# A quarter of the Q projection: plain matmuls in place of seven half-size products

## The chip, the cores and the metric

One core of one Trainium2 chip runs the whole program in a single launch. The metric is the device time in microseconds (us), given as the median of several executions. The engines are TensorE (PE in the profile, with its weight loads as PEld), VectorE (DVE), ScalarE (ACT), GpSimd (POOL), and SyncE (SP), whose queue issues most of the DMAs.

## The reference, cut to what matters

```python
x = A_x                                             # 1 x 2048 x 1024, bf16
# A: linear attention on layernorm(x), 32 heads of 32
q, k, v = split(layernorm(x) @ wqkv)                # wqkv 1024 x 3072
pq, pk = phi(q), phi(k)                             # phi(t) = (t + 1 if t > 0 else exp(t)) + 1e-6
kv = sum over tokens of pk * v ; z = sum over tokens of pk
o = (pq @ kv) / (pq . z + 1e-6)
h = x + o @ wo
# B: a two-layer MLP over the tokens of layernorm(h), with w1 (2048 x 3584), GELU, w2 (3584 x 2048)
out = h + B(layernorm(h))
```

The change lies in `q = layernorm(x) @ wq` and `pq = phi(q)` for 512 of the 2048 tokens, and in where intermediate sums are kept.

## The kernel before, in words

Tokens are handled in 16 tiles of 128; two tiles make a pair q = 0 to 7; four tiles make a block u = 0 to 3 of 512 tokens. The normalised tokens lie transposed in `xnT`.

**Seven products instead of eight.** For K of the pairs 2 to 7 and V of the pairs 1 to 7 (the rest of K and V is plain), a 256 x 1024 x 1024 product is done as a 2 x 2 block product with seven block multiplications (Strassen's scheme in Winograd's form). `Run` holds the seven, `p1` to `p7`; each is four matmuls of 128 x 512 into one PSUM bank. They need four sums of blocks of the weights (`w_sums`, t1 to t4, made once for each of K, V and Q) and four sums of blocks of the tokens (`x_sums`, s1 to s4, made for every pair); VectorE makes all of them. Product `p6` needs s2 and t2. ScalarE copies PSUM banks from one product to the next, and VectorE adds E, the bank of `p5`, to the banks after `p7` and `p3`.

**The rounds.** One round handles one pair: a K run, then a V run. `run_step` weaves the end of the run before (`p3`, `p4`) into the start of the next (`p1`, `p6`, `p2`, `p5`, `p7`). The same function fixes the order on VectorE and ScalarE: phi of a K result is two ScalarE instructions (`exp`, `relu`) and two on VectorE (`min` and `add`, then a sum). `late12` is the ScalarE pair and `dve12` the VectorE pair of the K result of `p3`. `after6` takes the layernorm statistics of a later token tile (`ln_stats`), `after5` finishes it (`ln_finish`: ScalarE `Ln` and `Exp`, VectorE `norm`, a transposing DMA), and `after7` makes the token sums of the next pair. An instruction given to `pin` stays behind the instruction traced before it on its engine; instructions without `pin` (the matmuls of `q_unit`, the memsets of `kv_ps`) are placed by the framework.

**Q.** For tokens 0 to 1023 and 1536 to 2047 the projection is plain: `q_unit` (in the rounds' gaps) and `q_held` (after the rounds) do one 128 x 512 block of Q with eight matmuls of 128 x 512, followed by the four instructions of phi. For tokens 1024 to 1535 (u = 2) two runs `QRun`, one for each half of the output columns, stand in round q = 5, each behind a K or V run. A `QRun` does seven products of eight matmuls of 128 x 256. Its four weight sums are made one by one on VectorE, behind the K runs of rounds 2 to 5 (`q_sums`). Its tokens come out in another order (`place`), and its phi of two of four results takes the relu on VectorE (`lean`).

**After the rounds.** The loop over `q_units[8:]` does the remaining plain Q blocks (16 here), and between them the denominators (`den`), their spreading over partitions through DRAM (`den_spread`), the folding of kv into wo (`fold`), the first weight loads and sums of B. Then the loop over the 16 token tiles seeds two PSUM banks with x (`seed`), adds the output matmuls (`out_mm`, 16 matmuls), copies and takes statistics (`out_evac`), and normalises (`normalize_h`). PSUM banks of these loops come in turn from a ring of five (`acc_tile`). The first banks of B (`psA`, `psB`) reuse the same memory.

Before, the sums of K lie in `shared_sb` (t2 to t4) and in place of one weight block (t1), those of V in `wo_sb` and likewise in place.

Of the kernel before, what the change touches and what calls it, by code (L numbers as in the profile page):

```python
# [10 lines left out]
P = 128  # L11
F32 = mybir.dt.float32
BF16 = mybir.dt.bfloat16
# [17 lines left out]
def kernel(  # L31
# [152 lines left out]
    def phi_parts(dst, src, n, pool, view=lambda t: t, lean=False):  # L184
        e_sb = pool.tile([P, n], BF16, tag="phi_e", name="e_sb")
        r_sb = None if lean else pool.tile([P, n], BF16, tag="phi_r", name="r_sb")

        def act():
            pin(nc.scalar.activation(e_sb[:], src, ACT.Exp))  # L189
            if not lean:  # L190
                pin(nc.scalar.activation(r_sb[:], src, ACT.Relu))

        def dve():
            pin(nc.vector.tensor_scalar(e_sb[:], e_sb[:], 1.0, PHI_EPS, ALU.min, ALU.add))  # L194
            if lean:
                pin(nc.vector.scalar_tensor_tensor(dst, view(src), 0.0, view(e_sb[:]), ALU.max, ALU.add))
            else:
                pin(nc.vector.tensor_tensor(dst, view(e_sb[:]), view(r_sb[:]), ALU.add))

        return act, dve  # L200
# [583 lines left out]
    with ExitStack() as actx:  # L784
        a3s = actx.enter_context(tc.tile_pool(name="a3s", bufs=4))
        hstat = actx.enter_context(tc.tile_pool(name="hstat", bufs=1))
        QT = ND // 2 * CW
        shared_sb = hstat.tile([P, 3 * QT + SW + (XRL + 1) * D], BF16, name="shared_sb")
        thirds = [shared_sb[:, i * QT:(i + 1) * QT] for i in range(3)]
        rd_sb = shared_sb[:, 3 * QT:3 * QT + SW].bitcast(FP16)  # L790
        xr_at = 3 * QT + SW
        xr_first = [shared_sb[:, xr_at + i * D:xr_at + (i + 1) * D] for i in range(XRL + 1)]
        assert (XRL + 1) * D >= 2 * QT
# [17 lines left out]
        with ExitStack() as a1:  # L811
# [7 lines left out]
            wo_parts = [wo_sb[:, 2 * t:2 * t + 2, :].rearrange("p a b -> p (a b)") for t in range(4)]  # L819

            def as_sums(flat):
                return [t.bitcast(FP16).rearrange("p (k c) -> p k c", c=CW) for t in flat]

            tv, tk = as_sums(wo_parts[0:3]), as_sums(thirds)
            tq = [
                t.bitcast(FP16).rearrange("p (k j f) -> p k j f", k=ND // 2, f=P)
                for t in (shared_sb[:, xr_at:xr_at + QT], shared_sb[:, xr_at + QT:xr_at + 2 * QT], wo_parts[3])
            ]
            spool = a1.enter_context(tc.tile_pool(name="spool", bufs=1))
# [101 lines left out]
            def with_sums(blocks, ts):  # L931
                return blocks, (blocks[1].bitcast(FP16), *ts)

            wq_b = wq_sb[:].rearrange("p (k two) (j par f) -> p k two j par f", two=2, par=2, f=P)
            kmov = with_sums(w_blocks(0), tk)
            vmov = with_sums(w_blocks(D), tv)
            qmov = with_sums([wq_b[:, :, k, :, c, :] for k in range(2) for c in range(2)], tq)

            def w_sums(mov, part):
                (b11, b12, b21, b22), (t1, t2, t3, t4) = mov  # L940
                for out, a, b in ((t3, b22, b12), (t1, b12, b11), (t2, b22, t1), (t4, b21, t2))[part]:
                    pin(nc.vector.tensor_tensor(out, a, b, ALU.subtract))

            xs_sb = spool.tile([P, 2, 4, hk2, P], FP16, name="xs")
# [5 lines left out]
            def x_sums(q, part=slice(0, 4)):  # L950
                a11, a12, a21, a22 = x_blocks(q)
                sm = xs_sb[:, q % 2]
                for out, a, b, op in (
                    (sm[:, 0], a21, a22, ALU.add), (sm[:, 1], sm[:, 0], a11, ALU.subtract),
                    (sm[:, 2], a11, a21, ALU.subtract), (sm[:, 3], a12, sm[:, 1], ALU.subtract),
                )[part]:
                    pin(nc.vector.tensor_tensor(out, a, b, op))  # L957

            class Run:
                def __init__(self, q, mov):  # L960
                    self.q = q
                    self.a11, self.a12, self.a21, self.a22 = x_blocks(q)
                    self.s1, self.s2, self.s3, self.s4 = (xs_sb[:, q % 2, t] for t in range(4))
# [82 lines left out]
            class KRun(Run):  # L1046
# [4 lines left out]
                lean = False  # L1051

                def view(self, t):
                    return t

# [3 lines left out]
                def evac(self, h, ps):  # L1059
                    self.phi[h, 0] = phi_parts(self.dst(h, 0), ps[:], CW, a2k, self.view)  # L1060
                    self.phi[h, 0][0]()

                def add(self, h, ps):
                    t = epool.tile([P, BANK], F32, tag="kt", name="kt")
                    pin(nc.vector.tensor_tensor(t[:], ps[:], self.E[:], ALU.add))
                    self.phi[h, 1] = phi_parts(self.dst(h, 1), t[:], CW, a2k, self.view, self.lean)
# [19 lines left out]
            class QRun(KRun):  # L1086
                lean = True

                def __init__(self, u, half):
                    self.u, self.half, self.phi = u, half, {}  # L1090
                    xv = xnT[:, :, u * SW:(u + 1) * SW].rearrange("p (k two) (r t f) -> p k two r t f", two=2, t=2, f=P)
                    self.a11, self.a12, self.a21, self.a22 = (xv[:, :, k, :, t, :] for t in range(2) for k in range(2))
                    self.s1, self.s2, self.s3, self.s4 = (
                        xs_sb[:, :, t].rearrange("p r k f -> p k r f") for t in range(4)
                    )
                    (self.b11, _, self.b21, self.b22), (self.t1, self.t2, self.t3, self.t4) = qmov

                def view(self, t):
                    return t.rearrange("p (j n) -> p j n", j=2)

                def mm(self, ps, lhs, rhs, start):
                    out = ps[:].rearrange("p (j r f) -> p j r f", j=2, f=P)
                    for j in range(2):
                        for k in range(hk2):
                            pin(nc.tensor.matmul(
                                out[:, j],
                                lhsT=rhs[:, k, 2 * self.half + j, :],
                                rhs=lhs[:, k],
                                start=(start and j == 0 and k == 0),
                                stop=(k == hk2 - 1),  # L1110
                                skip_group_check=True,
                            ))

                def dst(self, h, c):
                    n0 = self.u * SW + h * SW // 2
                    v = pqT[:, 4 * self.half:4 * self.half + 4, n0:n0 + SW // 2]
                    return v.rearrange("p (j two) n -> p j two n", two=2)[:, :, c, :]

            def run_step(n, prev, after6=None, after5=None, after7=None, fill=None, after3=None):
# [6 lines left out]
                if after3 is not None:  # L1126
                    after3()
# [11 lines left out]
                if n is not None:  # L1139
                    n.dve11()  # L1140
                if after5 is not None:
                    after5()
                if n is not None:
                    n.p7()
                prev.dve12()
# [115 lines left out]
            phi_dve((2, 0))  # L1261
            k_unit(2, 1)
# [16 lines left out]
            w_sums(kmov, slice(1, 3))  # L1279
# [3 lines left out]
            w_sums(vmov, slice(0, 1))  # L1283
# [5 lines left out]
            w_sums(vmov, slice(1, 3))  # L1289
# [13 lines left out]
            assert NSC == 4  # L1303
            q_units = [(u, j) for u in (0, 1, NSC - 1) for j in range(ND)]
# [17 lines left out]
            w_sums(kmov, slice(3, 4))  # L1322
            w_sums(vmov, slice(3, 4))
# [9 lines left out]
            q_sums = {2: slice(0, 1), 3: slice(1, 2), 4: slice(2, 3), 5: slice(3, 4)}  # L1333
            for q in range(2, NVP):
                runs = [KRun(q), VRun(q)]
                if q == 5:
                    runs = [runs[0], QRun(q // 2, 0), runs[1], QRun(q // 2, 1)]
                for n in runs:
                    kind = type(n).__name__[0]
                    i = {"K": 2 * q + 3, "V": 2 * q + 4}.get(kind, NS)  # L1340
# [5 lines left out]
                    def after5():  # L1346
                        if kind == "V":
# [6 lines left out]
                    def after7():  # L1354
                        if kind == "V" and q != 5 and q + 1 < NVP:
                            x_sums(q + 1)
                        if kind == "Q" and n.half == 1:
                            x_sums(q + 1, slice(0, 3))
                        if kind == "K" and q in q_sums:
                            w_sums(qmov, q_sums[q])  # L1360

                    def after3():
                        if type(prev) is QRun and prev.half == 1:
                            x_sums(q, slice(3, 4))

                    run_step(n, prev, after6, after5, after7, after3=after3)
                    prev = n
                if q == 6:
                    q_rows = wqkv_v.rearrange("p (k two) c -> p k two c", two=2)[:, :, 0, 0:D]
# [461 lines left out]
```

## Time and profile before

| what | value |
|---|---|
| median of 7 executions | 562.9 us (562.54 to 563.9) |
| the profiled execution: its own time, its span | 562.54 us, 560.8 us |
| TensorE busy | 552.4 us, 99% of the span, 3387 matmuls |
| TensorE weight loads busy | 320.2 us, 57% |
| VectorE busy | 441.9 us, 79% |
| ScalarE busy | 291.7 us, 52% |
| granted TensorE clock | 1.0 of full speed |
| chain that ended last | 85% TensorE, 5% VectorE, 2% ScalarE, 2% DMA |

The span runs from the first to the last instruction that the profile records; 1.7 us of the execution lie outside it. The end of a matmul is modelled: a line of four matmuls of 128 x 512 shows about 1.03 us although the next one can start 0.86 us after it. So the distance between two starts is what to read, and a waiting time that the profile shows on TensorE is shorter than the time lost.

The first 30 us load the first tokens and do the plain K and V, the rounds run from 41.5 to 138 us, the plain Q blocks from there to 179 us, the output projection to 235 us, and B from there to the end.

### The profile page before, as it was taken

How to read it: one execution, taken by the hardware profiler on the slowest of the kernel's cores; microseconds unless marked ns; L12 is line 12 of the kernel's file. 1: busy time of each engine (PE TensorE's matmuls, PEld its weight loads, DVE VectorE, ACT ScalarE, POOL GpSimd, SP SyncE). 2: the span in 40 equal slices, each digit the busy share in tenths (PEclk: the TensorE clock that was granted, in tenths of full speed). 3: DMA queues.
4: the chain of work that ended last, by engine and by line, in shares of the span. 5: the costliest groups of instructions: out<-in, count | busy, mean ns of one | idle time of the engine just before them, and what ended most of it. 6: DMA issues, size and time to landing. Idle time of an engine off the chain costs nothing.

```text
span 560.8 us, 8942 instructions
## 1 busy us (share of the span) xinstructions
PE 552.4 (99%) x3387; PEld 320.2 (57%) x3387; DVE 441.9 (79%) x858; ACT 291.7 (52%) x619; POOL 26.2 (5%) x36
## 2 busy tenths in 40 slices
PE   8999999999999999999999999999999999999997
PEld 3444446645444444456666666666444667667665
DVE  7798888664469689879989889897996879749746
ACT  5747767676677867645455565464310412413313
POOL 1000000000000000000000000000003103103111
PEclk9999999999999999999999999999999999999999
DMA  9933332310576992202240430413769659849434
GB/s 304 298 75 76 76 76 38 94 20 28 209 234 187 287 284 85 79 1 72 81 151 0 151 124 29 150 38 96 201 203 237 198 137 242 207 131 223 93 106 73
DMA packets 84443, 75.56 MB, mean 135 GB/s; under 512 B 15650, under 2 KB 76336, under 8 KB 84400
## 3 DMA queue, kind: packets, MB, share of 16 engines
q1 hardware_dynamic: 79632, 70.66, 42.2%
q0 software_dynamic: 4096, 3.68, 4.8%
q10 hardware_dynamic: 672, 0.66, 0.3%
q8 instruction: 26, 0.43, 0.3%
q14 instruction: 17, 0.14, 0.1%
HBM read 60.17 MB, written 11.67 MB: 128 GB/s over the span
## 4 chain that ended last, share of the span: by engine, by line
PE 85%; DVE 5%; ACT 2%; DMA 2%; issue 1%; DVEq 0%; ACTq 0%
PE psI L234 23%; PE psC L234 14%; PE acc_t L234 14%; PE psB L234 8%; PE psB L968 4%; PE psA L968 3%; PE psC L968 3%; PE psA L346 2%; PE psB L346 2%; PE acc_t L1294 2%; PE psE L968 2%; DMA wq<-in_B_w_dram 2%; PE psC L346 2%; PE psA L234 1%; PE psE L346 1%; DVE is L234 1%
## 5 line engine op out<-in xcount | busy, mean ns | idle before, releaser
L234 PEld LDWEIGHTS <-is 128*128 128x128 f16 x736 | 71.9, 98 | 31.6 <-DVE is L234 0.9
L234 PEld LDWEIGHTS <-sa 128*128 128x128 f16 x606 | 59.2, 98 | 27.5 <-issue 0.3
L234 PEld LDWEIGHTS <-wq 128*128 128x128 bf16 (+1 forms) x496 | 48.4, 98 | 28.9 <-issue 2.1
L234 PE MATMUL acc_t<-wo_sb,pqT 128*128 128x512 f16 x256 | 55.6, 379 | 0.0
L492 POOL DMA_DIRECT2D out_dram<-wq x28 | 24.4, 928 | 522.4 <-ACT wq L495 488.2
L234 PEld LDWEIGHTS <-pqT 128*128 128x128 bf16 x256 | 25.0, 98 | 30.5 <-issue 0.6
L234 DVE TENSOR_TENSOR t<-psI,t 128x256 f32<-128x256 f32 (+1 forms) x45 | 20.8, 475 | 22.2 <-PE psI L234 21.0
L234 PE MATMUL psC<-gs,wq 128*128 128x512 f16 x140 | 34.1, 379 | 0.0
L968 PEld LDWEIGHTS <-xs 128*128 128x128 f16 x208 | 19.7, 98 | 24.9 <-DVE xs L957 3.8
L194 DVE TENSOR_SCALAR e_sb<-e_sb 128x512 bf16<-128x512 bf16 x64 | 18.3, 286 | 19.1 <-ACT e_sb L189 19.0
L234 PE MATMUL psC<-hT,sa 128*128 128x512 f16 x112 | 31.2, 379 | 0.0
L234 PE MATMUL psI<-hi,is 128*128 128x256 f16 x200 | 30.0, 273 | 0.0
L234 PE MATMUL psB<-hT,sa 128*128 128x512 f16 x112 | 29.7, 379 | 0.0
L234 PE MATMUL acc_t<-xnT,wq_sb 128*128 128x512 bf16 x128 | 29.6, 379 | 0.0
L189 ACT ACTIVATE e_sb<-acc_t 128x512 bf16<-128x512 f32 x32 | 19.1, 597 | 18.7 <-PE acc_t L1294 9.4
L968 PE MATMUL psA<-wkv,xnT 128*128 128x512 bf16 x104 | 26.7, 379 | 0.0
L234 DVE BATCH_NORM_STATS2 hst<-acc_t 128x6 f32<-128x512 f32 x32 | 21.1, 689 | 6.4 <-ACT h_bf L234 6.4
L968 PEld LDWEIGHTS <-xnT 128*128 128x128 bf16 x156 | 15.3, 98 | 18.5 <-issue 0.8
L234 PE MATMUL psC<-hT,wq 128*128 128x512 f16 x96 | 24.6, 379 | 0.0
L234 DVE TENSOR_TENSOR e<-psI,es 128x256 f32<-128x256 f32 x20 | 8.5, 424 | 20.4 <-PE psI L234 20.4
L234 ACT COPY psI<-psI 128x256 f32<-128x256 f32 x50 | 18.0, 360 | 11.3 <-PE psI L234 9.4
L234 PE MATMUL psI<-gi,is 128*128 128x256 f16 x168 | 22.3, 273 | 0.4 <-DVE is L234 0.4
(242 smaller groups left out, 1129.8 us busy)
## 6 DMA issues: line engine op xcount, KB each, us to landing
wq<-in_B_w_dram SPq DMA_DIRECT2D x14, 1024.0 KB, 7.8
wq<-in_B_w_dram SPq DMA_DIRECT2D x12, 896.0 KB, 7.5
gs<-parked SPq DMA_DIRECT2D x9, 896.0 KB, 4.7
shared_sb<-rd_dram SPq DMA_DIRECT2D x32, 128.0 KB, 4.7
out_dram<-h_bf SPq DMA_DIRECT2D x16, 256.0 KB, 2.9
x_sb<-in_A_x_dram SPq DMA_DIRECT2D x15, 256.0 KB, 3.0
w2o<-in_B_w_dram SPq DMA_DIRECT2D x4, 896.0 KB, 10.7
out_dram<-wq POOLq DMA_DIRECT2D x28, 128.0 KB, 5.0
```

Of the source, the lines that this page charges most:

```text
L189: pin(nc.scalar.activation(e_sb[:], src, ACT.Exp))
L194: pin(nc.vector.tensor_scalar(e_sb[:], e_sb[:], 1.0, PHI_EPS, ALU.min, ALU.add))
L234: return (lambda *a, **kw: pin(op(*a, **kw))) if self.always or getattr(Held, self.key) else op
L346: pe.matmul(ps[:, cols], lhsT=lhs[:, k, :], rhs=mv(k)[:, cols], start=(start and k == 0), stop=(k == self.nk - 1), skip_group_check=True,)
L492: nc.gpsimd.dma_start(to, ot[:, a:b], accum_op=ALU.add)
L968: pin(nc.tensor.matmul(ps[:], lhsT=lhs[:, k, :], rhs=rhs[:, k, :], start=(start and k == 0), stop=(k == hk2 - 1), skip_group_check=True,))
L1294: nc.tensor.matmul(qp[:, 0:SW], lhsT=wq_sb[:, kt, j * P:(j + 1) * P], rhs=xnT[:, kt, u * SW:(u + 1) * SW], start=(kt == 0), stop=(kt == ND ...
```

## The change

The two `QRun` of round 5 go, with their four weight sums, the lean form of phi, the reordering of tokens and the DMA that reloads half of wq. The 512 tokens become eight more plain Q blocks in the loop after the rounds (24 in place of 16). The sums of K move to `pqT`, all four of V to `wo_sb`, so that no weight block is overwritten, and they are made in another order and at other places. In `run_step`, `dve12` moves from behind `p7` to a place ahead of `after5`. The buffers of reciprocals and of x get pools of their own. Denominators, spreads, scalings and the first loads of w1 get other places in the two loops after the rounds.

```diff
-            tv, tk = as_sums(wo_parts[0:3]), as_sums(thirds)
...
+            tv = wo_sb[:].rearrange("p (t a) (b c) -> p t (a b) c", t=4, c=CW).bitcast(FP16)
+            tk = pqT[:, ND - 4:ND, :].rearrange("p t (b c) -> p t b c", c=CW).bitcast(FP16)
...
-                for out, a, b in ((t3, b22, b12), (t1, b12, b11), (t2, b22, t1), (t4, b21, t2))[part]:
+                for out, a, b in ((t1, b12, b11), (t2, b22, t1), (t3, b22, b12), (t4, b21, t2))[part]:
                     pin(nc.vector.tensor_tensor(out, a, b, ALU.subtract))
...
-            class QRun(KRun):
...
                 prev.late12()
                 if n is not None:
                     n.dve11()
+                prev.dve12()
                 if after5 is not None:
                     after5()
                 if n is not None:
                     n.p7()
-                prev.dve12()
                 if after7 is not None:
                     after7()
...
             phi_act((2, 0))
             phi_dve((2, 0))
+            w_sums(kmov, slice(1, 2))
             k_unit(2, 1)
...
             ln_finish(G0)
-            w_sums(kmov, slice(1, 3))
+            w_sums(vmov, slice(0, 2))
             proj_unit(0, NDC + 1, pin)
             ln_stats(G0 + 1)
             proj_unit(1, NDC, pin)
-            w_sums(vmov, slice(0, 1))
+            w_sums(vmov, slice(2, 4))
             proj_unit(1, NDC + 1, pin)
             ln_finish(G0 + 1)
             x_sums(1)
             for b in range(NKB):
                 nc.vector.memset(kv_ps[b][:], 0.0)
-            w_sums(vmov, slice(1, 3))
...
-            q_units = [(u, j) for u in (0, 1, NSC - 1) for j in range(ND)]
+            q_units = [(u, j) for u in range(NSC) for j in range(ND)]
...
             v1.p6()
             v1.p2()
-            w_sums(kmov, slice(3, 4))
-            w_sums(vmov, slice(3, 4))
+            w_sums(kmov, slice(2, 4))
...
-                runs = [KRun(q), VRun(q)]
-                if q == 5:
-                    runs = [runs[0], QRun(q // 2, 0), runs[1], QRun(q // 2, 1)]
-                for n in runs:
...
+                for R in (KRun, VRun):
+                    n = R(q)
...
-                        if kind == "K" and q in q_sums:
-                            w_sums(qmov, q_sums[q])
...
-            sums_at, ahead = (9, 11, 12, 13, 15), first_sums()
-            scale_at = {7: (0, 0), 8: (0, 1), 14: (1, 0)}
+            sums_at, ahead = (11, 13, 17, 19, 21), first_sums()
+            scale_at = {7: (0, 0), 8: (0, 1), 15: (1, 0), 16: (1, 1), 23: (2, 0)}
...
-                if n in (1, 3, 9):
-                    den({1: 0, 3: 2, 9: 1}[n])
-                if n in (1, 9):
-                    den_spread(n // 9)
+                if j == 1:
+                    den(u - 1)
+                    den_spread(u - 1)
...
-                if n in (2, 3, 10, 11):
+                if n in (4, 5, 10, 11):
                     load_w1(n // 10, n % 2, pin)
...
-            scale_at = {0: (1, 1), 4: (2, 0), 5: (2, 1), 8: (3, 0), 9: (3, 1)}
+            scale_at = {0: (NSC - 2, 1), 6: (NSC - 1, 0), 8: (NSC - 1, 1)}
...
-                if i in (1, 5):
-                    den_spread(2 + i // 5)
+                if i == 2:
+                    den_spread(NSC - 1)
```

## The prediction

> **What bounds the kernel now.** The page gives TensorE 99% of the span, so I read next who makes TensorE wait, over the whole span (line waited for, releaser: us in total, times, longest):
>
> ```profile
> engine line waited for: us in total, times, longest us
> PE psB L968 <- DVE xs L957: 1.6, 4, 0.4
> PE acc_t L98 <- DVE warm L88: 1.2, 1, 1.2
> PE psA L234 <- DVE hst L234: 0.5, 1, 0.5
> PE psI L234 <- DVE is L234: 0.4, 1, 0.4
> PE psC L968 <- DVE kt L1065: 0.3, 1, 0.3
> ```
>
> The list is short: what TensorE has to stream sets the time, and a few waits add to it, most of them `p6` waiting for the token sum s2. TensorE's timeline gives prices and places (start us, us, ...):
>
> ```profile
> 69.94 1.03 PE L968 MATMUL psC<-wo_sb,xnT 128*128 128x512 f16 x4
> 71.35 1.04 PE L968 MATMUL psB<-shared_sb,xs 128*128 128x512 f16 x4 [0.38 <-DVE xs L957]
> 72.22 1.03 PE L968 MATMUL psA<-wkv,xnT 128*128 128x512 bf16 x4
> ...
> 91.87 1.04 PE L1105 MATMUL psA<-xnT,wq_sb 128*128 128x256 bf16 x8
> 92.74 1.04 PE L1105 MATMUL psE<-xs,wq_sb 128*128 128x256 f16 x8
> ...
> 140.28 5.34 PE L1294 MATMUL acc_t<-xnT,wq_sb 128*128 128x512 bf16 x24
> ```
>
> Starts of dense groups of four lie 0.864 us apart; from 69.94 to 71.35 it is 1.41. So each such wait costs 0.55 us, not the 0.38 shown. Eight 128x256 matmuls take 0.87 us (91.87 to 92.74); 24 plain ones take 5.18 us (140.28 to the next group's start at 145.46), 215.8 ns each.
>
> **Part 1, the stream.** Removed: 2 runs x 7 products x 0.8725 us (mean over the listed groups) = 12.21 us. Added: 8 blocks x 8 matmuls x 0.2158 = 13.81 us. Sum **+1.60 us**, on the path: from 145 to 235 us the starts of TensorE show no hole. Beside it, hidden: the phi of eight blocks needs 1.0 us of ScalarE and 0.7 of VectorE per 1.73 us of TensorE (rows between 145 and 150 us, where both wait for TensorE). Should that cover fail, the five-bank ring would fill first, and then what ScalarE needs beyond 1.73 us would be TensorE's loss, block by block.
>
> A sentence of the skill disagrees here: the Trainium skill, "TensorE: Matmul & The Clock Gate", "Back-to-back issue gap", gives a sustained 131 ns per matmul at 512 columns and 81 at 128. By it, as an estimate, the added matmuls would cost 8.4 us and the removed 9.1 to 14.7 us, so this part would be -0.7 to -6.3 us; the trace shows 215.8 ns and 109 ns at a clock of 1.0, and decides.
>
> **Part 2, the rounds.** Three rounds end in that wait (57.77, 71.35, 84.93 us), and at 115.86 `p4` waits for VectorE, 0.48 us by the same count, behind the second QRun. Together 3 x 0.55 + 0.48 = 2.13 us. Why is s2 late? VectorE, then ScalarE, in the round that ends at 71 us:
>
> ```profile
> 67.30 0.21 DVE L859 BATCH_NORM_AGGREGATE mv<-st 128x2 f32<-128x12 f32 x1
> 68.69 0.55 DVE L866 TENSOR_SCALAR xn<-x_sb,mv,rstd 128x1024 bf16<-128x1024 bf16 x1 [1.19 <-ACT rstd L863]
> 69.16 0.69 DVE L1039 TENSOR_TENSOR vaug<-psC,e 128x512 bf16<-128x512 f32 x1
> 69.76 0.28 DVE L194 TENSOR_SCALAR e_sb<-e_sb 128x512 bf16<-128x512 bf16 x1
> 70.07 0.42 DVE L198 TENSOR_TENSOR pk<-e_sb,r_sb 128x512 bf16<-128x512 bf16 x1
> 70.42 0.42 DVE L957 TENSOR_TENSOR xs<-xnT 128x512 f16<-128x512 bf16 x1
> 70.87 0.42 DVE L957 TENSOR_TENSOR xs<-xs,xnT 128x512 f16<-128x512 f16 x1
> ```
>
> ```profile
> 67.09 0.63 ACT L189 ACTIVATE e_sb<-kt 128x512 bf16<-128x512 f32 x1
> 67.62 0.62 ACT L191 ACTIVATE r_sb<-kt 128x512 bf16<-128x512 f32 x1
> 68.14 0.28 ACT L862 ACTIVATE lnv<-mv,eps_ln 128x1 f32<-128x1 f32 x1
> 68.46 0.20 ACT L863 ACTIVATE rstd<-lnv 128x1 f32<-128x1 f32 x1
> ```
>
> VectorE idles 1.19 us for `rstd`, then does norm, the add of `p7`, `dve12` (69.76 and 70.07) and only then s1 and s2. The change puts `dve12` into the idle stretch. Its first half can start at 67.76 (exp ends 67.72), its second at 68.28 (relu ends 68.24, 0.04 later as elsewhere in the rows) and gives way after 0.35, at 68.63; `rstd` lets norm go at 68.69. What is queued behind the new waits is norm, the add, the token sums; none moves back, since norm waits for two later ScalarE instructions anyway. The sums then follow the add at 69.76, 0.66 us earlier, so s2 lets `p6` go at 71.35 - 0.66 = 70.69; TensorE is free for it at 69.94 + 0.864 = 70.80. The wait closes with 0.11 to spare. Next late would be the add of `p7`, ready at 69.85 for a `p4` that starts at 69.94 in both versions. The removed sum of Q's weights (1.22 us behind each K run) widens VectorE's room before the idle stretch, not the spare after it. Round 5, dense before with QRuns in it, becomes an ordinary round and is taken as dense. I take **-2.13 us**; the bounds are that and +0.07 (waits of 0.55 at four round ends instead of the 2.13).
>
> The skill's rule that VectorE's queue is strictly first in, first out (Trainium skill, "TensorE: Matmul & The Clock Gate", "Architectural detail: the array is 16× 32×32, not 1× 128×128") speaks against moving waits ahead of norm: alone it would charge norm the 0.5 us or so that `dve12` waits for ScalarE; with the rows above it charges nothing.
>
> **Part 3, the start.** At 33.61 TensorE ends the first kv sums; three Q matmuls run from 34.01, `p6` of the first V run starts at 35.26, released by s2 (34.78 to 35.20), and at 43.25 `p4` is 0.09 late. Lost: 0.40 + 0.60 + 0.09 = 1.09 us. VectorE is full from 26.15 to there; it carries five weight sums of 1.14 to 1.26 us ahead of s2 in that stretch. The change moves one to 19.5 us, where VectorE idles 0.8 + 0.2 + 0.2 + 0.3 us for ScalarE, and norm at 26.15 waits for ScalarE either way. So s2 ends about 1.1 us earlier and `p6` can start near 34.15: 0.54 lost instead of 1.00. The later 0.09 stays (VectorE's queue to that add holds the same instructions). **-0.46 us**; bounds -1.09 (all holes closed) and +0.7 (one sum of 1.2 us falls ahead of s2 after all, less the part gained).
>
> **Part 4, the seam at 235 us.** `psA` waits for `hst`: the statistics of the last tile's first bank (234.74 to 235.43) free the bank that B's first product takes; TensorE was done at 235.11 and starts at 235.57. Ring places: 16 Q + 1 + 16 fold + 32 seeds = 65 banks before, so the last tile holds calls 64 and 65, places 4 and 5 of five. After: 73, the last tile holds calls 72 and 73, places 2 and 3. `psA`'s bank then belongs to an earlier tile, if places keep their banks. Its other input, the normalised tile, is done at 234.82. **-0.44 us**; bounds 0 and -0.46.
>
> **Part 5, taken at nothing.** The spread of block 2's reciprocals has 6 blocks (10.4 us) and the phi of the last (about 2.2 us) between its denominator and its scaling. In the trace the first one takes 151.41 - 149.00 to the write, first issue at 153.13, fourth half a microsecond per issue later at 154.5, then 4.7 us median to land: 10.2 us, 14.2 with the longest landing (8.7). VectorE may then wait 1.6 us; two output tiles (6.9 us of TensorE) lie between that and TensorE. w1 is issued behind the same spreads as before and used no earlier. Two scalings (1.13 us each) leave the output loop, which is dense already: nothing.
>
> **Sum:** +1.60 - 2.13 - 0.46 - 0.44 = -1.43 us. The profiled execution took 562.54 (span 560.8, 1.7 outside), giving 561.1; it was the fastest of seven, 0.36 below the median, so I forecast 562.9 - 1.43 = **561.5 us**, own range 560.8 (the start closes wholly) to 561.8.
>
> **Rivals.**
> *Only part of it:* the rounds close, but the start or the seam or both give nothing: -0.97, -0.99 or -0.53 us, 561.9 to 562.4. For it: the start's order on TensorE is partly placed by the framework, and banks in the ring may change places. Within 0.2% (1.13 us), about what a measurement of this kernel can tell from no change.
> *Slower, the waits stay:* s2 remains late at four round ends because `dve12`, placed ahead, does not fit into the idle stretch. The spare is 0.06 us at norm and 0.11 us at `p6`; from 0.66 us of delay on, nothing is gained. Then +1.60 + 0.07 - 0.46 = +1.2 us, 564.1, with the seam as it is. Against it: each of these instructions follows TensorE and ScalarE by fixed steps, and TensorE's steps shrink only after s2.
> *Slower, a late spread:* VectorE is held at the scaling of block 2; from some 7 us on, TensorE runs out of seeded banks; 10 us late would cost 3: +1.6, 564.5. Against it: the landings above.
> *No effect:* parts 1 and 2 cancel as -0.53 shows; it is in the first rival.
>
> **Chances.** Forecast 0.43 (faster); part of it 0.32 (within 0.2%); waits stay 0.20 and late spread 0.05 (slower). Range 560.7 to 564.2: from the forecast with the whole start closed to the waits that stay, each with 0.1 for the runs' scatter; the late spread is left out.
>
> **What would show it.** Part 1: 64 more 128x512 matmuls on `wq_sb`, no 128x256 ones before 235 us, the Q blocks 13.8 us longer. Part 2: no TensorE wait on `xs` in the rounds, 13.03 us from round to round (as now from 120.26 to 133.29) in place of 13.58 (57.77 to 71.35), `dve12` ahead of norm and no idle stretch over 0.9 us there. Part 3: the first V run's `p6` near 34.15. Part 4: no wait of `psA` on `hst`. I am wrong if waits on `xs` remain or if a hole opens between 138 and 235 us.

## The result, and the profile after

The changed kernel takes 560.26 us (median of 14 executions, 560.03 to 562.41); the kernel before, timed beside it, 562.96 us (37 executions). The ratio is 0.9954, 95% interval 0.9945 to 0.9963: 2.7 us less, where 1.4 was forecast. The profiled execution took 561.53 us with a span of 559.8. A second profile of each kernel, taken on one chip, gave 560.33 us (span 558.6) and 562.76 us (561.0).

Where the time went is read by cutting both TensorE timelines at groups that both kernels have, and subtracting starts (us, first profiles):

| stretch of TensorE | before | after | difference | forecast |
|---|---|---|---|---|
| start to `p1` of the first V run | 30.09 | 31.60 | +1.51 | 0 |
| to `p6` of the first K run | 14.11 | 13.57 | -0.54 | -0.46 |
| to the plain Q blocks after the rounds | 96.08 | 81.72 | -14.36 | -14.34 |
| to the output loop | 42.85 | 56.67 | +13.82 | +13.81 |
| to B's first product (`psA`) | 52.44 | 51.81 | -0.63 | -0.44 |
| B | 325.23 | 324.43 | -0.80 | 0 |

The fourth row of the forecast is the added stream; the third is the removed stream (12.21) and the waits (2.13). The first row is the landing of the first loads in that one execution: in the second pair of profiles it is +0.24 (30.19 against 30.43), and the other stretches are as here (B: 325.32 against 324.41). The sum without it is -2.51. ("B" is the two-layer MLP, from its first product to the end of the span.)

TensorE's waits over the whole span after (engine, line waited for: us in total, times, longest) answer to the first list of the prediction:

```profile
PE acc_t L98 <- DVE warm L88: 1.2, 1, 1.2
PE tp L1113 <- DVE xn L849: 1.1, 2, 1.0
PE acc_t L870 <- DMA wkv<-in_A_wqkv_dram: 0.9, 1, 0.9
PE psB L946 <- DVE xs L932: 0.3, 1, 0.3
```

The second and third line are that execution's start. Of the four waits on `xs` one is left, at the start; those of `psA`, `psI` and `kt` are gone. In TensorE's timeline the groups that stood 1.41 us apart now stand 0.86 apart, and the 24 plain matmuls have their old price (5.18 us to the next group's start at 132.07):

```profile
70.37 1.03 PE L946 MATMUL psC<-wo_sb,xnT 128*128 128x512 f16 x4
71.23 1.03 PE L946 MATMUL psB<-pqT,xs 128*128 128x512 f16 x4
...
126.89 5.34 PE L1232 MATMUL acc_t<-xnT,wq_sb 128*128 128x512 bf16 x24
```

VectorE in the same round, to be laid beside its rows in the prediction (start us, us, instruction, idle before it and who ended it):

```profile
68.18 0.29 DVE L193 TENSOR_SCALAR e_sb<-e_sb 128x512 bf16<-128x512 bf16 x1 [0.76 <-ACT e_sb L189]
68.70 0.42 DVE L194 TENSOR_TENSOR pk<-e_sb,r_sb 128x512 bf16<-128x512 bf16 x1 [0.23 <-ACT r_sb L190]
69.12 0.55 DVE L849 TENSOR_SCALAR xn<-x_sb,mv,rstd 128x1024 bf16<-128x1024 bf16 x1
69.58 0.69 DVE L1017 TENSOR_TENSOR vaug<-psC,e 128x512 bf16<-128x512 f32 x1
70.19 0.41 DVE L931 TENSOR_TENSOR xs<-xnT 128x512 f16<-128x512 bf16 x1
70.63 0.42 DVE L932 TENSOR_TENSOR xs<-xs,xnT 128x512 f16<-128x512 f16 x1
```

The two instructions of `dve12` (68.18 and 68.70) lie in the stretch that was idle before, the norm at 69.12 has no wait of its own left, and the sums follow the add of `p7` directly. s2 ends at 71.05; before, `p6` started 0.06 us after the end of s2 (71.29, 71.35), so it could start at 71.11 here, and TensorE is free at 71.23.

**B, which was taken as unchanged, is 0.8 us shorter.** B of before has two holes (VectorE, then TensorE):

```profile
514.34 0.62 DVE L234 TENSOR_TENSOR is<-wq 128x896 f16<-128x896 bf16 x1 [0.95 <-DMA wq<-in_B_w_dram]
```

```profile
515.68 0.94 PE L234 MATMUL psI<-gi,is 128*128 128x256 f16 x7 [0.42 <-DVE is L234]
...
523.60 2.10 PE L234 MATMUL psB<-gT,sa 128*128 128x512 f16 x9 [0.17 <-ACT psB L531]
```

From start to start they cost 0.59 and 0.35 us, with 0.06 more at 521.73 between them; against that, the changed kernel loses 0.08 us early in B (the group at 243.88 starts 1.17 us after a group of five, which takes 1.08 when dense), as do all runs without the wait of `psA`, and its span ends 0.08 later behind the last matmul. VectorE makes the sum `is` from a block of w2 that SyncE's queue loads, and the block is late. The same rows after have no wait:

```profile
513.21 0.61 DVE L230 TENSOR_TENSOR is<-wq 128x896 f16<-128x896 bf16 x1
```

```profile
515.00 0.93 PE L230 MATMUL psI<-gi,is 128*128 128x256 f16 x7
```

Of the pair of loads issued at 502 and 504 us (times to landing: shortest, median, longest) the second is meant; first before, then after:

```profile
DMA to landing us min/median/max: 5.7/7.7/9.8
```

```profile
DMA to landing us min/median/max: 5.5/6.6/7.8
```

### The profile page after: what moved, and what is told of

Same layout as the page of the kernel before. It is cut to its first block, busy times and chain, and to the rows that moved or that the text cites. A ratio compares the mean times of both kernels' runs of the same rounds, so it can differ in the third digit from the quotient of the medians.

```text
span 559.8 us, 8830 instructions
## 1 busy us (share of the span) xinstructions
PE 552.5 (99%) x3339; PEld 315.9 (56%) x3339; DVE 435.9 (78%) x850; ACT 290.9 (52%) x617; POOL 26.2 (5%) x36
## 4 chain that ended last, share of the span: by engine, by line
PE 95%; DVE 2%; DMA 2%; SPq 1%; issue 0%; ACT 0%; DVEq 0%
PE psI L230 25%; PE acc_t L230 18%; PE psC L230 16%; PE psB L230 8%; PE psB L946 4%; PE psC L946 4%; PE psA L946 4%; PE psB L342 2%; PE psA L342 2%; PE acc_t L1232 2%; PE psE L946 2%; PE psC L342 2%; DMA x_sb<-in_A_x_dram 2%; PE acc_t L870 2%; PE psA L230 1%; PE kvps L899 1%
## 5 line engine op out<-in xcount | busy, mean ns | idle before, releaser
L230 PE MATMUL acc_t<-xnT,wq_sb 128*128 128x512 bf16 x192 | 43.4, 379 | 0.0
L189 ACT ACTIVATE e_sb<-acc_t 128x512 bf16<-128x512 f32 x40 | 23.9, 597 | 24.5 <-PE acc_t L230 12.0
L230 PEld LDWEIGHTS <-wq_sb 128*128 128x128 bf16 x192 | 18.5, 98 | 23.0 <-issue 1.3
L230 ACT CAST h_bf<-acc_t 128x512 bf16<-128x512 f32 x32 | 18.4, 581 | 11.9 <-PE acc_t L230 11.5
## 6 DMA issues: line engine op xcount, KB each, us to landing
w2o<-in_B_w_dram SPq DMA_DIRECT2D x4, 896.0 KB, 10.4
```

Source lines behind the costliest of these rows:

```text
L230: return (lambda *a, **kw: pin(op(*a, **kw))) if self.always or getattr(Held, self.key) else op
```

## The experiments

Each was run beside the kernel before on one chip; "B" is the time from B's first product to the end of the span, and costs of holes are distances between starts. The theory at the outset was the prediction's for the rounds, the start and the seam; for B there was none yet.

### Both kernels once more

> The kernel before, looked at once more, for the two places that the prediction did not name. In its first profile two holes in B, 0.59 us at 515.7 and 0.35 us at 523.6, follow a weight load that took 9.8 us to land. Theory (chance of the landing): this load lands in under 8.9 us in some executions, and then both holes are gone and the stretch from B's first matmul to the end is about 0.8 us shorter, 324.4 us. Rival (the layout of the kernel before makes the load slow): it lands after more than 8.9 us again and the stretch takes 325.2 us. The first V run's p6, the three rounds and the seam should show the same waits as in the first profile.

> The changed kernel, looked at once more. In its first profile TensorE reached the second plain V projection 1.5 us later than before (22.96 against 21.44 us), behind a weight load that landed late (0.86 us) and a token load (0.99 us). Theory (chance of the landing): this time it is there by about 21.5 us and the span is about 558.3 us. Rival (the change moved the first loads): 23 us again and a span near 559.8. B from its first matmul to the end: 324.4 us by the theory of chance or by the rival of the layout; if it is 325.2 here, the layout is no cause.

Measured: 562.76 and 560.33 us. In the kernel before every wait of the first profile is there again, B's holes with 0.67 and 0.34 us; in the changed kernel B has none again, and of the start's waits the one for the weight load (0.9 us) is gone. So what differs in B is not chance of one execution.

### The early phi alone, in the kernel before

```diff
                 n.dve11()
+            prev.dve12()
             if after5 is not None:
                 after5()
             if n is not None:
                 n.p7()
-            prev.dve12()
```

> The kernel before with one edit: dve12 ahead of after5, as in the change. Theory (the place of dve12 makes the waits of the rounds): no wait on xs at the ends of rounds 2 to 4, -1.65 us there; behind the second QRun the lean phi (0.28 + 0.69 us) now stands ahead of norm and the add, so that p4 of the K run waits some 0.5 us longer than the 0.48 of before: -1.1 us in all, ratio 0.998. Rival (the 1.22 us weight sums of Q make them late): waits stay, ratio 1.000 to 1.001.

Measured: 562.14 us against 562.85, ratio 0.9988 (0.9979 to 0.9997), 0.7 us instead of the 1.65 of three waits. The three waits on `xs` are gone, as the theory has it. But behind the second `QRun` `p4` waits longer: 1.06 us lost in place of 0.48, as expected; 0.44 at 95.40, behind the first, is new and was not expected.

```profile
115.61 1.02 PE L968 MATMUL psC<-shared_sb,xnT 128*128 128x512 f16 x4 [0.89 <-DVE kt L1065]
```

VectorE in front of it, in the same run:

```profile
113.81 0.69 DVE L196 SCALAR_TENSOR_TENSOR pqT<-kt,e_sb 128x512 bf16<-128x512 f32 x1
114.42 0.54 DVE L866 TENSOR_SCALAR xn<-x_sb,mv,rstd 128x1024 bf16<-128x1024 bf16 x1
114.87 0.68 DVE L1065 TENSOR_TENSOR kt<-psC,e 128x512 f32<-128x512 f32 x1
```

Here VectorE has almost no idle stretch (0.27 us before norm in the kernel before), and the lean phi's second half takes 0.69 us instead of 0.42. Moved ahead, it delays the add that `p4` needs. Behind the first `QRun` the moved pair waits 0.58 and 0.22 us for ScalarE, and the add (94.67) stands behind it. So the move gains its full amount only where the add has to wait for norm anyway; with the QRuns it gives back about 1.0 of 1.65 us. That is a dependence between two parts of the change which the prediction had priced apart.

### The changed kernel without the early phi

The reverse of the diff above, in the changed kernel.

> The changed kernel with one edit undone: dve12 back behind p7. Theory (the place of dve12 makes the waits): the wait on xs comes back at the ends of rounds 2 to 6 where a norm stands ahead, 4 to 5 waits of 0.55 us, +2.2 to +2.7 us against the changed kernel, so about the time of before. Rival (the weight sums of Q made them): no wait on xs in the rounds, time of the changed kernel, ratio 0.995 to the kernel before.

Measured: 562.32 us, ratio to before 0.9992 (0.9983 to 1.0001), 2.1 us more than the changed kernel. Waits of 0.55 us on `xs` are back at four round ends, 57.61, 71.20, 84.79 and 98.37 us:

```profile
71.20 1.04 PE L946 MATMUL psB<-pqT,xs 128*128 128x512 f16 x4 [0.38 <-DVE xs L932]
```

Four times 0.55 is 2.2 us. This is the state of the slower rival ("the waits stay"), whose four waits were counted rightly; its total of 564.1 us was 1.8 too high; the seam and B, which gained too, are 1.4 of it.

### K's sum t2 put back, in the changed kernel

```diff
             phi_dve((2, 0))
-            w_sums(kmov, slice(1, 2))
             k_unit(2, 1)
...
             ln_finish(G0)
+            w_sums(kmov, slice(1, 2))
             w_sums(vmov, slice(0, 2))
```

> The changed kernel with K's sum t2 made where it was before, behind the layernorm of the ninth token tile instead of ahead of the last plain K units. Theory (VectorE's queue to the token sum s2 sets the start of p6 of the first V run): s2 and that p6 come 1.1 us later, the stretch from the first V run's p1 to K(2)'s p6 takes 14.1 to 14.7 us in place of 13.57, the kernel 560.8 to 561.4. Rival (the gain at the start came from elsewhere, such as the places that the framework chose for the memsets or the Q matmuls): no change, 560.3.

Measured: 561.29 us, 1.0 more than the changed kernel. The stretch from the first V run's `p1` to K's `p6` takes 14.56 us (30.16 to 44.72) in place of 13.56. VectorE ends s2 at 35.29 instead of 34.34 in the changed kernel's second profile, though its norm ahead of the weight sums starts earlier (26.23 against 26.50). `p6` of the first V run in that second profile, then in this run:

```profile
34.41 1.04 PE L946 MATMUL psB<-wo_sb,xs 128*128 128x512 f16 x4 [0.28 <-DVE xs L932]
```

```profile
35.35 1.04 PE L946 MATMUL psB<-wo_sb,xs 128*128 128x512 f16 x4 [0.89 <-DVE xs L932]
```

The theory of the start stands: counted from that norm, one weight sum ahead of s2 makes s2 1.22 us later. TensorE lost 1.00 of it; a Q matmul of 0.22 us ran in the meantime.

### The PSUM ring turned, both ways

In the kernel before the ring of five banks is turned by four places ahead of the loop of plain Q blocks, so that the last tile no longer holds the bank that B takes first; in the changed kernel it is turned by three at the same place, so that it does.

```diff
+            acc_ring[:] = acc_ring[4:] + acc_ring[:4]
```

> The kernel before with one edit: the ring of five PSUM banks is turned by four places ahead of the loop of plain Q blocks, so that the last output tile no longer lies in the bank that B's first product takes. Theory (the seam's wait comes from that bank alone): psA no longer waits on hst, and the 0.63 us between its start and a dense one are gone: 562.3 us, ratio 0.9989. Rival (another input is due at the same time, the normalised tile or the statistics): psA waits again by as much, ratio 1.000.

> The changed kernel with its ring of five PSUM places turned by three ahead of the output loop, so that the last token tile's first bank is again the one that B's first product takes, as before. Theory: the wait of psA on hst at 235 us is back, psA starts 0.6 us later after the same start of the output loop, the kernel takes 560.8 to 560.9. Rival (the seam closed because of something else, such as the earlier scalings): no wait there, 560.3.

Measured: in the kernel before the wait of `psA` on `hst` is gone and the time 562.66 us against 563.02, ratio 0.9991 (0.9982 to 0.9999). In the changed kernel it is back, 0.63 us from start to start, and the time is 560.9 us. First the kernel before, as it was and with its ring turned, then the changed kernel with its ring turned:

```profile
235.57 2.75 PE L234 MATMUL psA<-hE,wq 128*128 128x512 f16 x12 [0.46 <-DVE hst L234]
```

```profile
235.27 2.97 PE L234 MATMUL psA<-hE,wq 128*128 128x512 f16 x13
```

```profile
234.39 1.46 PE L230 MATMUL psA<-hE,wq 128*128 128x512 f16 x6 [0.46 <-DVE hst L230]
```

From the output loop to `psA` the kernel before now takes 51.81 us, as the changed one did, and the changed one 52.44. So the wait at the seam comes from the place in the ring. B's holes at 515 and 523 us stayed in the kernel before (0.61 and 0.34), so the seam does not make them. In the profile of the changed kernel with the turned ring holes of 0.59 and 0.34 us appeared at 475 and 483 us, around another load (below).

### Is it the number of DMAs? Two runs that say no

B's late load had a first theory: the kernel before issues one DMA more (the reload of half of wq), and later DMAs might then fall on other resources. So the changed kernel got that reload, and the kernel before one more small DMA.

```diff
+                if q == 6:
+                    q_rows = wqkv_v.rearrange("p (k two) c -> p k two c", two=2)[:, :, 0, 0:D]
+                    nc.sync.dma_start(wq_sb[:].rearrange("p (k two) c -> p k two c", two=2)[:, :, 0, :], q_rows)
```

> The changed kernel with one DMA added: the reload of half of wq behind round 6 that the kernel before has (it writes the values that lie there already). All later DMAs of the SP queue are then as many as before. Theory (the number of DMAs ahead sets how long the weight load at 504 us takes to land): it lands after 9.7 us or more instead of 8, the two holes in B come back, B takes 325.2 instead of 324.4 us, +0.8 us against the changed kernel: 561.1. Rival (something else in the kernel before delays that load): B takes 324.4 us, no difference to the changed kernel.

```diff
+                    nc.sync.dma_start(b1_rows[:], B_b1.rearrange("(t p) -> t p", p=P))
```

> The kernel before with one small DMA added behind the reload of wq (it loads b1 again, 28 rows of 256 bytes). Theory (the number of DMAs ahead sets the landing, odd or even): the load at 504 us lands in about 8 us as in the changed kernel, the two holes in B vanish, 562.0 us. Rival 1 (a larger count matters, or the size of the reload): the holes stay, 562.9. Rival 2 (chance): neither this nor the added reload in the changed kernel shows a pattern.

Measured: 560.06 us with the reload, the load lands after 8.0 us, B 324.36, no hole. 563.03 us with the small DMA in the kernel before; the load lands after 10.4 us and the holes are 1.23 and 0.34 us. The theory fell: neither run moved the landing the way it said.

### Is it the fetching of code? Two runs that shift it

The trace lists every packet that the 16 DMA engines move. On queue q8, of kind "instruction", there are 26 packets of 16 KB in both kernels, about 1 us each, one per some 260 of TensorE's 6,700 to 6,800 instructions (matmuls and weight loads). In the stretch from 505 to 513 us, the queues of before end with two lines that the changed kernel does not have there:

```profile
q8 instruction: 1, 0.02, 0.8%
q14 instruction: 1, 0.01, 0.2%
```

Before, the packet on q8 comes at 510.8 us, while the load of 504.5 is in flight; after it comes at 513.1, when the load has landed. The changed kernel executes 48 matmuls (with 48 weight loads) fewer ahead of B, so TensorE's code runs out at other places. Theory: the fetch in flight delays the load. To shift the fetches alone, the ten warm-up matmuls on zeros in the first 6 us became sixty narrow ones in the changed kernel (ninety in the combined kernel below); they feed no product.

```diff
-        for t in range(n):
-            mm(warm[:, 0:P], warm[:, 0:BANK])
+        for t in range(6 * n):
+            mm(warm[:, 0:P], warm[:, 0:80])
```

> The changed kernel with its ten idle-time warm-up matmuls of 512 columns replaced by sixty of 80 columns, so that TensorE executes 50 more matmuls (100 more instructions) before anything else and each later fetch of TensorE's code falls earlier in B. Theory (a fetch of code inside the flight of the second weight load of the pair near 504 us delays that load): the fetch at 513 us moves to about 510 us, the load lands after 9.4 to 10.4 us in place of 7.8, the wait of psI on the sum is is back, about 0.6 us, and that of psB on ScalarE, about 0.35; B takes 325.1 to 325.4 us in place of 324.4, and the kernel some 0.8 us more than the changed one (561.0, if the start is as long as before). Rival (the hole hangs on something else in which the two kernels differ: memory places, where loads are issued, the number of DMAs): the load lands after 7.8 to 8.3 us, no hole, B 324.4.

Measured: the fetch moved from 512.2 (second profile of the changed kernel) to 506.2 us, the load of 503.3 lands after 10.2 us in place of 8.1, and the holes are there, 0.95 and 0.34 us. First the two loads, then the rows:

```profile
DMA to landing us min/median/max: 5.6/7.9/10.2
```

```profile
513.47 0.62 DVE L230 TENSOR_TENSOR is<-wq 128x896 f16<-128x896 bf16 x1 [1.32 <-DMA wq<-in_B_w_dram]
```

```profile
514.81 0.94 PE L230 MATMUL psI<-gi,is 128*128 128x256 f16 x7 [0.79 <-DVE is L230]
```

B took 325.77 us in place of 324.41, and B's first product started as before (234.23 against 234.19). The profiled execution took 561.74 us, 1.4 more. The median of twelve executions was 562.62, from 561.32 to 565.33; why seven of them lie above 562.3 stays open, since none of them was profiled. The holes account for the profiled execution, not for the median.

### The combination

The kernel before keeps its QRuns and gets the sums in places of their own (so nothing is overwritten and no reload is needed), the changed kernel's order of the weight sums at the start, the early phi except behind a QRun, the add of `p7` ahead of norm where a K run follows a QRun, and the turned ring.

```diff
...
+            behind_q = type(prev) is QRun
+            if not behind_q:
+                prev.dve12()
+            add_first = behind_q and type(n) is KRun
+            if add_first:
+                n.p7()
             if after5 is not None:
                 after5()
-            if n is not None:
+            if n is not None and not add_first:
                 n.p7()
-            prev.dve12()
+            if behind_q:
+                prev.dve12()
...
+            acc_ring[:] = acc_ring[4:] + acc_ring[:4]
```

> Both kernels' gains together: the two QRuns of before with their four weight sums, but the sums kept apart (K's in the parts of pqT for tokens 512 to 1023 and 1536 to 2047, V's in wo_sb, Q's in shared_sb), so that no weight block is overwritten and no reload is needed; the order of the first sums and the early dve12 of the change (late only behind a QRun, and the add of p7 ahead of norm there); the ring turned as in the other run. Theory (the terms add): the changed kernel less the stream's 1.60 us, 558.7 us, ratio 0.9926. Rival (VectorE has no room for Q's sums once the waits are gone): waits on xs or kt come back, 559.5 to 561.

> The combined kernel (QRuns kept, sums apart, early phi) with its ten warm-up matmuls of 512 columns replaced by ninety of 56 columns, 80 more matmuls: the fetches of code, now at 451, 470, 489 and 510 us inside four weight loads, move some 12 us earlier, to 439, 458, 477 and 498, between them. Theory: the loads issued at 440.4, 462.3, 480.6 and 502.9 land 1 to 2 us sooner (8.0 to 8.4 for the one at 462, 7.8 to 8.3 for the one at 503), the holes at 473, 481 and 521 us go, B takes 324.4 to 324.8 us in place of 326.1, and the kernel 558.0 to 558.4. Rival (the fetches don't matter): B 325.3 to 326.1, 559.4.

Measured for the combination: **559.45 us** (559.04 to 560.64), ratio to before 0.9940 (0.9928 to 0.9952), the fastest kernel of the study. B's first product starts at 232.77 us, 1.4 earlier than in the changed kernel's second profile, which is the 1.60 of the stream less 0.44 that `p4` still loses behind a QRun at 94.54, plus a start 0.27 shorter. B takes 326.13 us, with holes of 0.66 at 473.54, 0.34 at 481.46 and 0.35 at 521.62, and one that the profile does not show as a wait: `psI` starts 1.07 us after the group ahead of it, 0.21 more than dense.

```profile
512.62 1.03 PE L234 MATMUL psC<-gs,wq 128*128 128x512 f16 x4
513.69 0.94 PE L234 MATMUL psI<-gi,is 128*128 128x256 f16 x7
```

The profiled execution took 560.64 us, the longest of the five, so its holes need not be in the others.

With the fetches shifted it is 560.7 us: slower, against what was expected. Its start is 1.55 us longer (TensorE waits 1.2 us for a normalised tile near 17 us); whether that is the narrow warm-up or the landing of the first loads was not tried. B takes 325.18, 0.95 less. The load of 504.2 now has no fetch on q8 inside and lands after 8.3 us; the holes at 513 and 521 are gone, as the theory had it. But the load of 463.9, also without such a fetch, lands after 9.6 us, and its hole stays, 0.38 us at 474.80 and 0.35 behind it.

### All fourteen profiles, by the two loads

| load | fetch on q8 in flight | landing after, us | hole of `psI` |
|---|---|---|---|
| of 503 to 505 us | yes: 7 profiles | 9.4 to 10.4 | 7 of 7, from 0.21 us |
| of 503 to 505 us | no: 7 profiles | 7.8 to 8.5 | none |
| of 462 to 466 us | no, or in its last 0.3 us: 12 profiles | 8.0 to 8.5 in ten, 9.6 and 9.8 in two | those two |
| of 462 to 466 us | yes: 2 profiles | 8.6 and 9.9 | the one of 9.9 |

At the later load the fetch in flight and the late landing go together in 14 of 14 profiles, and the two runs that moved the fetch moved the landing with it. At the earlier load they do not. So: a landing later than about 9 us goes with the hole in all 10 cases (least, 0.21 us, in the combination, where TensorE was already 1.1 us late), and one of up to 8.6 us in none of 18. The packet on q14, which stands beside q8's in the view above, is a rival: it too is in flight in all seven late landings of the later load. But in the combination with shifted fetches it comes at 510.9 us with q8's gone, and the load lands after 8.3; and in the changed kernel with shifted fetches it comes 8.8 us after the load's issue, when the load of the changed kernel had landed. For one load, then, the late landing hangs on where q8's fetch falls; how a packet of 1 us delays a load by 1 to 2 us is not shown, and what made the landing late at 464 us in two runs without such a packet stays open. There too the DMA engines are full: in all fourteen profiles two output writes are issued on GpSimd's queue with that load and two more 2.9 and 3.4 us later.

## Why the prediction was right in its direction and too small in its size

- **Part 1, the stream, right.** +1.60 was forecast; the rounds and the Q blocks together (-14.36 + 13.82) differ by 0.01 from the forecast's -14.34 + 13.81. The page's 131 ns, weighed there, does not hold for this stream: the eight added blocks cost 215.8 ns a matmul. The same section of the page (Trainium skill, "TensorE: Matmul & The Clock Gate", "Back-to-back issue gap") has a formula for an isolated matmul, columns/2.4 + 2.5 ns; by it, as an estimate, 512 columns are 215.8 ns and 256 are 109.2, and those are the spacings measured in these dense groups (215.8 and 109).
- **Part 2, the rounds, right** in mechanism and size, -2.13. `p6` starts 0.86 us behind the group ahead of it, s2 in time by the margin that was worked out (0.12 us, where 0.11 was forecast). That it holds only where no QRun stands is shown by the early phi alone in the kernel before. The prediction took the removal of the 0.48 at 115.86 for certain, and it was; it did not say that the removal of the QRuns is what lets the early phi pay in full.
- **Part 3, the start, right:** -0.46 forecast, -0.54 measured. The 0.09 at 43.25 stayed, as said, and 0.45 of the wait remains at `p6`.
- **Part 4, the seam, right** in its mechanism (both ring runs), and mis-sized: -0.63, not -0.44, and outside the bounds given (0 and -0.46). The term was read from 235.57 less 235.11, the end of TensorE's last group. But that end is modelled; starts of dense groups give 0.63. The prediction had warned of just this for part 2 and then did not apply it here.
- **Part 5, at nothing, right:** VectorE's scalings wait for no reciprocal in the profile after; the late spread did not come.
- **The step that failed is one that is not in the sum: B was taken as unchanged.** The list of waits showed `psI` waiting for `is`, 0.4 us, one time, and the prediction quoted it and gave it no term. It belonged to a weight load that landed after 9.8 us; in the changed kernel that load lands after 7.8, and the wait is gone along with 0.35 behind it: B is 0.80 us shorter, which no part had. The trace of before alone does not say that the load would land sooner; but a wait for a DMA that lands late by a little, in a stretch that the change shifts in time, should have been held as a term with bounds: -0.94 (both holes go) and, as the holes at 475 us in the changed kernel with the turned ring showed later, as much the other way. The low end of 560.7 would then have been 559.8.

Sum measured: -2.51 by the stretches, -2.70 by the medians; of the 1.1 to 1.3 us beyond the forecast 0.80 is B, 0.19 the seam, 0.08 the start. The rest is within the scatter of the start.

None of the rivals came true. "The waits stay" named the waits that count: they come back in the changed kernel without the early phi, and cost 2.1 us.

## What to carry to other kernels

A stretch that a change does not touch is still shifted against its transfers and against the fetching of code, so each wait for a DMA in the list of waits needs a bound in the sum, also when it lies 280 us behind the edit. Losses on TensorE are read from start to start, at every wait, not at the first one only; one of 0.21 us was in no list of waits. An instruction moved into an idle stretch is free only in the rounds that have that stretch: in the kernel before, one move gained 1.65 us in three rounds and gave about 1.0 back behind two runs where the next add then waited for it. And what a removal is worth is found by keeping the removed part and fixing its waits: with the seven products kept the kernel takes 559.45 us, 0.8 less by the medians than with the plain blocks that replaced them (the intervals of the two ratios overlap; in the profiles B starts 1.4 us earlier).

## What the hardware showed that was not expected

- Code is fetched through the same DMA engines: 26 packets of 16 KB and about 1 us each on q8 and, in the changed kernel, 18 of 8 KB on q14 over the span. In flight beside an 896 KB weight load while output writes fill the engines, one went with a landing after 9.4 to 10.4 us instead of 7.8 to 8.5 at one load, more than its own 1 us, and not at another. Trainium skill, "DMA: Bandwidth & Descriptors", "Issuing engines are not separate DMA queues", says that DMAs started by ScalarE, SyncE or GpSimd end up on the same 16 DMA engines and interleave. The profile agrees in that it counts SyncE's q1 (65%), GpSimd's q0 (37%) and the code's q8 (0.8% of the stretch from 505 to 513 us) against the same 16 engines; no view here shows a single engine.
- Fifty more narrow matmuls in the first 6 us cost nothing there (B's first product at 234.23 against 234.19) and, in the one profile taken, went with 1.36 us more in B, 500 us later.
- A load issued at the same time behind B's first product (229.4 to 229.6 us behind it in all fourteen profiles) landed after 8.0 to 9.9 us, with equal writes beside it. What decides is open for that load.
